# Moving the head-pair interleave of batches 3 and 4 from GpSimd to VectorE, behind the third output tile

## The chip, the cores and the metric

One core of a Trainium2 chip. The metric is the device time of one execution in microseconds (us). The engines are TensorE (PE, its weight loads PEld), VectorE (DVE), ScalarE (ACT), GpSimd (POOL), and the sync engine's queue (SP), which starts most stores.

## The reference

Attention with a decay bias over 8 batches of 8 heads, then an MLP with a gelu on the 4608 resulting tokens.

```python
scores = scale * np.matmul(q, k.transpose(0, 1, 3, 2))          # 8 x 8 x 576 x 576, head size 64
scores = np.where(causal, -1e9, scores + np.minimum(bias, 0.0)) # bias from a cumulated sum of s
attn = softmax(scores)
x = np.matmul(attn, v)   # rearranged to [4608, 512]
h = x @ w_in             # [4608, 2048]
out = gelu(h) @ w_out    # [4608, 512], float32
```

## The kernel before

The program runs in chunks c = 0 to 8 of 512 tokens; I call chunk c "stage c". Stages 1 to 6 do the MLP of chunk c and, woven into its second half, the attention of batch c + 1. They also prepare batch c + 2: its q and k come in as bf16 (`early`), are rearranged so that the two heads of a pair lie side by side (`interleave`), are stored to DRAM as rows, and are read back by transposing DMAs into `qkT`.

```python
def interleave(b, n):
    ...
    for j in range(2):
        (nc.gpsimd if b < 5 else nc.vector).tensor_copy(        # L180: 128 x 1152 bf16
            t[:, j].rearrange("g r e d -> g e r d"),
            early[b, n][:, j].rearrange("g e (r d) -> g e r d", r=G),
        )

# in stage c >= 1, nb = c + 1, pairs p of heads
late = int(c == 1)
for p in range(1, NP):
    if nb + 1 < B and p == 1 + late:
        interleave(nb + 1, "q"); write_rows(nb + 1, 0, nc.sync)
    if nb + 1 < B and p > 1 and not late:
        transpose_rows(nb + 1, p - 2)
    sc_item(nb, p)          # scores (L387), exp on ScalarE (L403), causal masks on VectorE (L412, L417)
    av_item(nb, p - 1)      # avd, avn (L425); ln on ScalarE (L441, L442); xT on VectorE (L461)
    l2_item(c, p, 0, 12)    # 24 o_ps matmuls (L544)
    if p == NP - 1:
        ...                 # the transposes left over, then:
        av_item(nb, p); norm_rest(nb)
    l2_item(c, p, 12)       # 8 more, then o_sb <- o_ps on VectorE (L551) and the store
    if nb + 1 < B and p == 1 + late:
        interleave(nb + 1, "k"); write_rows(nb + 1, 1, nc.sync)
```

The names: P is exp of a pair's scores, and its mask must be done before `avd` and `avn`, the sums over P (denominator and numerator) that give `xT`, the MLP's input; h_ps and o_ps are the MLP's first and second matmul. In front of `avd` of pair 1 or 2 stand 32 o_ps matmuls (24 and then 8 of one output tile); in front of `avd` of pair 3 only 24.

## Time and profile before

| | before |
|---|---|
| time, the three runs known before the prediction | 333.27 us median (333.2 to 333.33) |
| the profiled run | 331.73 us, span 329.8 |
| TensorE busy | 315.5 us, 96% of the span |
| VectorE, GpSimd busy | 194.6 us, 78.7 us |
| stage 1, 2, 3 in the profile | 35.29, 36.91, 34.05 us |

The profile's page gives busy times, groups of instructions by source line ("L412"), and the chain of work that ended last. A stage is measured from its first h_ps matmul to the next stage's, as the chain has them (in stage 1 this is the first one behind a wait for xT; four stand before it). Idle time counts only where it holds up TensorE.

### The profile page before, as it was taken

What the parts mean: (1) busy time and instruction counts of PE and PEld (TensorE: products, weight loads), DVE (VectorE), ACT (ScalarE), POOL (GpSimd) and SP (SyncE); (2) the same over time, 40 slices, a digit from 0 to 9 for tenths busy, and PEclk for the clock granted to TensorE, in tenths of its full rate; (3) what the DMA queues carried; (4) which work ended last, traced back from release to release, by engine and by line L of the source; (5) the groups of instructions that cost most, each with busy time, mean ns of one, the idle gap of its engine ahead of it and who ended that gap; (6) DMA issues with size and microseconds to landing.
All of it is one profiled execution on the core that took longest, in us unless ns stands there. A gap on an engine that the chain in (4) does not pass through costs nothing.

```text
span 329.8 us, 8731 instructions
## 1 busy us (share of the span) xinstructions
PE 315.5 (96%) x3755; PEld 182.8 (55%) x3755; DVE 194.6 (59%) x368; ACT 205.0 (62%) x292; POOL 78.7 (24%) x112
## 2 busy tenths in 40 slices
PE   7999998999999996999999999999999999999992
PEld 3566555666655554556655565556555655455552
DVE  5776548994589348937495658745783663150021
ACT  3796849668666855577676767677759676104400
POOL 8744254305610555007102500230000000000000
PEclk9999999999999999999999999999999999999998
DMA  7999999854975599977997995585410110010012
GB/s 111 219 208 213 231 196 265 248 107 65 273 229 113 96 230 215 181 123 224 252 150 136 211 293 104 96 242 177 109 34 34 54 45 2 34 65 34 1 66 72
DMA packets 53837, 47.45 MB, mean 144 GB/s; under 512 B 31328, under 2 KB 43872, under 8 KB 53792
## 3 DMA queue, kind: packets, MB, share of 16 engines
q0 software_dynamic: 15936, 23.07, 38.4%
q1 hardware_dynamic: 37856, 23.75, 28.6%
q8 instruction: 31, 0.51, 0.7%
q14 instruction: 14, 0.11, 0.1%
HBM read 36.85 MB, written 16.52 MB: 162 GB/s over the span
## 4 chain that ended last, share of the span: by engine, by line
PE 88%; ACT 4%; DVE 3%; issue 2%; DMA 1%; POOL 0%; DVEq 0%; POOLq 0%
PE h_ps L522 38%; PE o_ps L544 35%; PE sc_ps L387 5%; PE avn L425 3%; PE avd L425 3%; ACT P L403 2%; DMA early_q<-in_k_dram 1%; PE o_ps L565 1%; DVE qkT L372 1%; PE avr L425 1%; DVE xT L461 1%; PE tr_ps L366 1%; ACT ln L441 1%; ACT ln L442 1%; PE avw L425 0%
## 5 line engine op out<-in xcount | busy, mean ns | idle before, releaser
L544 PE MATMUL o_ps<-w_out_r,gT 128*64 128x512 bf16 x1120 | 129.3, 380 | 0.0
L522 PE MATMUL h_ps<-xT,w_in_r 128*64 128x512 bf16 x1152 | 126.2, 379 | 0.6 <-DVE xT L461 0.6
L522 PEld LDWEIGHTS <-w_in_r 128*64 128x64 bf16 x1152 | 68.5, 110 | 56.3 <-issue 1.1
L544 PEld LDWEIGHTS <-gT 128*64 128x64 bf16 x1120 | 61.0, 110 | 49.9
L529 ACT ACTIVATE gT<-h_ps 128x1024 bf16<-128x1024 f32 x54 | 54.3, 1023 | 53.9 <-PE h_ps L522 53.9
L403 ACT ACTIVATE P<-sc_ps 128x1024 bf16<-128x1024 f32 x64 | 62.0, 1021 | 26.4 <-PE sc_ps L387 24.7
L412 DVE TENSOR_TENSOR P<-P,tri_bf 128x512 bf16<-128x512 bf16 x58 | 29.5, 516 | 45.7 <-ACT P L403 45.3
L551 DVE COPY o_sb<-o_ps 128x512 f32<-128x512 f32 x33 | 22.7, 688 | 49.1 <-PE o_ps L544 49.1
L215 DVE TENSOR_REDUCE amx<-qkT 128x2 f32<-128x1152 bf16 x32 | 40.9, 1334 | 0.0
L204 POOL DMA_DIRECT2D raw_v<-in_v_dram x40 | 34.3, 880 | 7.8 <-DMA w_in_r<-in_moe_w_in_dram 2.0
L461 DVE SCALAR_TENSOR_TENSOR xT<-avn,ln 128x256 bf16<-128x256 f32 (+3 forms) x66 | 22.4, 385 | 19.6 <-ACT ln L442 14.7
L232 DVE TENSOR_TENSOR vv<-raw_v,wb 128x512 bf16<-128x512 f32 (+3 forms) x44 | 25.1, 631 | 0.0
L441 ACT ACTIVATE ln<-avd 128x256 f32<-128x256 f32 x58 | 19.2, 391 | 8.6 <-PE avd L425 8.6
L222 DVE TENSOR_REDUCE amv<-raw_v 128x1 f32<-128x2048 f32 (+1 forms) x16 | 23.0, 1469 | 2.5 <-DMA raw_v<-in_v_dram 2.5
L442 ACT ACTIVATE ln<-ln 128x512 f32<-128x512 f32 (+1 forms) x40 | 23.5, 587 | 1.3
L532 ACT ACTIVATE gT<-h_ps 128x512 bf16<-128x512 f32 x36 | 19.6, 602 | 6.3 <-PE h_ps L522 6.3
L387 PE MATMUL sc_ps<-qkT 64*128 64x256 bf16 (+2 forms) x320 | 21.1, 250 | 1.3 <-ACT P L403 0.5
L387 PEld LDWEIGHTS <-qkT 64*128 64x128 bf16 x320 | 12.9, 94 | 15.7 <-issue 12.4
L425 PEld LDWEIGHTS <-wb 128*64 128x64 bf16 x384 | 17.1, 110 | 6.5 <-issue 3.0
L425 PEld LDWEIGHTS <-vv 128*64 128x64 bf16 x384 | 17.7, 110 | 3.3 <-DVE xT L461 1.6
L425 PE MATMUL avd<-P,wb 128*64 128x256 bf16 x232 | 16.7, 263 | 2.0 <-DVE P L412 2.0
L666 POOL CAST pace<-qkT 128x1 f32<-128x1 bf16 x4 | 0.8, 196 | 69.0 <-DMA qkT<-rows 69.0
(101 smaller groups left out, 179.6 us busy)
## 6 DMA issues: line engine op xcount, KB each, us to landing
out_dram<-o_sb SPq DMA_DIRECT2D x35, 256.0 KB, 3.5
raw_v<-in_v_dram POOLq DMA_DIRECT2D x32, 256.0 KB, 9.5
rows<-qk_bf SPq DMA_DIRECT2D x12, 576.0 KB, 6.6
early_q<-in_q_dram POOLq DMA_DIRECT2D x13, 288.0 KB, 10.5
early_k<-in_k_dram POOLq DMA_DIRECT2D x13, 288.0 KB, 11.6
w_in_r<-in_moe_w_in_dram POOLq DMA_DIRECT2D x4, 512.0 KB, 11.6
w_out_r<-in_moe_w_out_dram POOLq DMA_DIRECT2D x4, 512.0 KB, 15.1
raw_v<-in_v_dram POOLq DMA_DIRECT2D x8, 128.0 KB, 9.9
```

What stands on the lines that cost most here:

```text
L204: nc.gpsimd.dma_start(out=t[:n_st, st, :, :], in_=bass.AP(tensor=v.tensor, offset=v.offset + b * H * S * D + st * 128 * D, ap=[[D, n_st], ...
L215: nc.vector.tensor_reduce(amx[:, b * NP + p], qkT[b % 2][:, :, p, :S], axis=AX, op=ALU.max, apply_absolute_value=True)
L232: eng.tensor_tensor(vb[:n_st, st0:st1, h0:h1, :], t[:n_st, st0:st1, h0:h1, :], wb[:n_st, st0:st1, b * H + h0 : b * H + h1] .unsqueeze(3).t ...
L387: nc.tensor.matmul(s_ps[:, e, off : off + n], lhsT=qkT[b % 2][e * 64 : e * 64 + 64, 1, p, jt * 128 : jt * 128 + 128], rhs=qkT[b % 2][e * 6 ...
L403: nc.scalar.activation(P[:, :, UO[u] : UO[u] + UW[u]], s_ps[:, :, : UW[u]], func=AF.Exp, scale=scale)
L412: eng.tensor_tensor(d, d, tri_bf.unsqueeze(1).unsqueeze(1).to_broadcast([128, 2, 2, 128]), op=MULT)
L425: nc.tensor.matmul(out[e * 64 : e * 64 + 64, lo : lo + n], lhsT=(wb[:, jt, b * H + h : b * H + h + 1].to_broadcast([128, 64]) if den else ...
L442: nc.scalar.activation(ln[:, :w], ln[:, :w], func=AF.Exp, scale=-1.0)
L461: nc.vector.scalar_tensor_tensor(out if p1 - p0 > 1 else out[:, 0], cut(num), math.exp(-LNC[c]), cut(ln), op0=MULT, op1=MULT,)
L522: nc.tensor.matmul(h_of[c, f2][i][e * 64 : e * 64 + 64], lhsT=w_in_r[:, ko, ft * 128 + e * 64 : ft * 128 + e * 64 + 64], rhs=xT[:, ko, c * ...
L529: nc.scalar.activation(gT_of[c][:, f2 * 2 : f2 * 2 + 2, :], hh_of[c, f2], func=AF.Gelu)
L544: nc.tensor.matmul(o_ps[e * 64 : e * 64 + 64], lhsT=gT[:, ft, t0 : t0 + 64], rhs=w_out_r[:, ft, :], start=(ft == 0), stop=(ft == FT - 1), ...
```

## The change

The intent is to take the copies of batches 3 and 4 off GpSimd, put them on VectorE at a point where it has time and the data have landed, and gather the DMA transposes behind the row stores.

```diff
-            (nc.gpsimd if b < 5 else nc.vector).tensor_copy(
+            (nc.gpsimd if b == 2 else nc.vector).tensor_copy(
...
-            late = int(c == 1)
+            late = c < 3
             for p in range(1, NP):
-                if nb + 1 < B and p == 1 + late:
+                if nb + 1 < B and p == 1 and not late:
                     interleave(nb + 1, "q")
                     write_rows(nb + 1, 0, nc.sync)
...
+                if nb + 1 < B and p == 2 and late:
+                    interleave(nb + 1, "q")
+                    write_rows(nb + 1, 0, nc.sync)
                 if nb + 1 < B and p == 1 + late:
                     interleave(nb + 1, "k")
                     write_rows(nb + 1, 1, nc.sync)
```

## The prediction

> **What bounds the kernel now.** I read the page first (busy shares, then the chain that ended last), then the windows by stage, then the chain and the timelines of the two stages that the change touches. The stages are the chunks c of the MLP; a stage starts at its first h_ps matmul (L522).
>
> ```profile
> PE 315.5 (96%) x3755; PEld 182.8 (55%) x3755; DVE 194.6 (59%) x368; ACT 205.0 (62%) x292; POOL 78.7 (24%) x112
> ...
> PE 88%; ACT 4%; DVE 3%; issue 2%; DMA 1%; POOL 0%; DVEq 0%; POOLq 0%
> ```
>
> TensorE is busy 96% of the span and carries 88% of the chain of waits. VectorE at 59% is not the bound. So only a stretch in which TensorE stands still can be won, and all of the standing still together is 329.8 - 315.5 = 14.3 us. The next table says where in the steady part it is (columns: stretch, length, busy time of each engine, clock, DMA share, GB/s). The stretches are stages c=1, 2, 3 and 5.
>
> ```profile
> 59.21:94.50 35.29, 34.51 (x422) 22.20 (x423) 25.88 (x44) 24.62 (x36) 13.07 (x16) 1.00 0.78 186
> 94.50:131.41 36.91, 34.43 (x394) 19.30 (x392) 24.67 (x36) 23.88 (x35) 13.95 (x19) 1.00 0.81 162
> 131.41:165.46 34.05, 34.05 (x395) 19.39 (x392) 21.81 (x39) 23.36 (x34) 7.03 (x10) 1.00 0.91 196
> ...
> 199.58:233.62 34.04, 34.04 (x394) 19.35 (x392) 22.01 (x41) 23.87 (x35) 4.44 (x6) 1.00 0.65 156
> ```
>
> Stages 3 and 5 do the same matmuls as stage 2 (394 or 395) in 34.05 us without a gap; they interleave their next batch on VectorE. Stage 2, which interleaves batch 4 on POOL, takes 36.91, so 36.91 - 34.05 = 2.86 us more. Stage 1 (batch 3 on POOL) has 35.29 - 34.51 = 0.78 us without a matmul; the rest of its surplus over 34.05 is work of its own, 28 more matmuls. The clock is 1.00 in all.
>
> The chain inside stage 2 and the timelines of POOL and VectorE there tell what the 2.86 us are:
>
> ```profile
> 124.04 0.95 DVE P L412
> 124.99 3.59 issue
> 128.58 0.41 DVE P L412
> 128.99 0.14 DVE P L417
> 129.13 0.68 DVE xT L461 x2
> 129.81 0.04 issue
> 129.85 0.57 PE avn L425 x8
> ```
>
> ```profile
> 123.97 2.24 POOL L180 COPY qk_bf<-early_q 128x1152 bf16<-128x1152 bf16 x2
> 126.14 2.22 POOL L180 COPY qk_bf<-early_k 128x1152 bf16<-128x1152 bf16 x2
> ```
>
> ```profile
> L412 DVE TENSOR_TENSOR P<-P,tri_bf x58: 405/425/4616, 14.7 to 264.1; 128x512 bf16<-128x512 bf16 x58
> ```
>
> The causal mask of head pair 3 (L412, median 425 ns) starts at 124.04, 0.07 us after the first POOL copy, and lasts 4616 ns, until 128.66; the four POOL copies end at 128.36. So one mask stood behind all four. TensorE then waits 2.04 us for the mask and 0.45 us for xT behind it. In stage 1 the same thing happened more mildly: the two k copies ran from 89.64 to 92.07, and within them the mask L412 at 89.98 took 1.08 us instead of 0.42 and L417 at 90.99 took 1.16 instead of 0.22. The q copies from 86.39 to 88.63 met only L461 and L551, which read PSUM, and slowed neither.
>
> [...] the blocked operations are L412 and L417 (two SBUF inputs, 4616 and 1161 ns at most), and L551 out of PSUM keeps 693 ns at most. [...] the trace has 450 to 462 as medians of L180 on VectorE. [...] the trace has 1151 ns for the same copy, 2.5 times VectorE's. [...] of VectorE's first q copies, one took 890 ns at 150.7, as POOL began to issue raw_v (150.79).
>
> **The change, part by part.**
>
> It removes 8 of the 12 POOL copies (batches 3 and 4): 8 x 1.15 = 9.2 us of POOL, none of it on the chain by itself; on the chain is what they block. It leaves the four of batch 2 (56.0 to 60.6), where a mask of 1.04 us and one of 1.16 stay slow, so that loss stays.
>
> It adds 8 copies on VectorE, four in stage 1 and four in stage 2, behind the o_sb copy of the third output tile:
>
> ```profile
> L180 DVE COPY qk_bf<-early_q x6: 450/462/890, 150.7 to 219.2; 128x1152 bf16<-128x1152 bf16 x6
> L180 DVE COPY qk_bf<-early_k x6: 449/452/491, 155.2 to 223.7; 128x1152 bf16<-128x1152 bf16 x6
> ```
>
> A pair of them takes 0.85 us on the timeline (155.18), as they overlap a little, so four take about 1.65 us.
>
> Stage 2. The o_sb copy ends at 123.35. The early tiles of batch 4 were issued from 111.12 to 113.12, the last landed 8.9 us later at 122.0, so nothing is waited for. Copies: 123.3 to 124.95. Masks, which without that would start at 124.04 and 124.95: 124.9 to 125.3 and 125.25 to 125.65, L417 until 125.8. Next comes xT of pair 2 (L461), which can't start before ScalarE's ln, 125.51 + 0.63 = 126.14. So the copies fit into time in which VectorE waits anyway, with about 0.35 us to spare; one slow copy (890) would use it up exactly. The matmul that needs the mask starts behind 24 o_ps matmuls, at 126.77. The stage should thus shrink to the 34.05 us of stage 3: a gain of 2.86, and I take 2.8.
>
> Stage 1. The o_sb copy ends at 88.38; q copies until 89.2. The last k piece was issued at 79.7 and landed 9.8 us later, at 89.5, so VectorE stands in front of k for 0.4 us. k copies: 89.55 to 90.4. Masks: 90.4 to 91.15, L417 to 91.3, xT from 91.3 (ln is ready at 91.17) to 92.1, in three pieces that took 0.81. Before, xT ended at 92.88 and avn started at 92.93. avn cannot start before its avd matmuls end, some 92.0. Gain: 92.93 - 92.15 = 0.78; with a doubt about the wait for k, I take 0.7.
>
> What moves: the row stores. Stage 1 stores k at 90.5 instead of 92.10, stage 2 stores q and k at about 124.3 and 125.2 instead of 126.24 and 128.40. In stage 2 the eight DMA transposes go together after the rows. Before, they started at 134.09, were split by a store, and the last landed by 150.26, when the pace copy on POOL ran. With k rows landing 9.8 us after 125.2 they start near 135 less the earlier shift, take some 10 to 11 us as in stage 1 (11.17), and the first pair is there by 139. The first score matmul of batch 4 was at 146.09 and will be near 142.6. It holds. The loads behind the pace copy in stage 2 move up by some 1.5 us: no cost.
>
> Sum: 2.8 + 0.7 = 3.5 us. Nothing later waits for VectorE (stages 3 to 6 have no gap), so it carries to the end: 333.27 - 3.5 = 329.8 us, 1.05% less.
>
> **The rivals.**
>
> 1. VectorE becomes the wait. Behind the third tile there is only the slack above. If [...] a tile lands late, masks slip by as much as 1 us and pair 3 starts late. For: a copy of 890 ns at 150.7, and early_k(3) landing at 89.5. Against: stages 3 to 5 carry two copies before each mask group without a gap, and POOL has no DMA issue near 88. It would leave a gain of 1.5 to 2.7: 330.6 to 331.8 us.
> 2. The gathered transposes come too late for stage 3 or block the output stores in the sync queue. For: transposes run one after another, 8 in 11.17 us. Against: rows are stored earlier than before, and three o_sb buffers covered a store held until 139.48. If it held, stage 3 would stand for 1 to 3 us, and the time would be 331 to 333.
> 3. [...] the stretched mask came from something else (say its input). Against: it ended 0.3 us after the last POOL copy, and stages with no POOL copy show none. It would leave 333.
>
> **Range and chances.** The mechanism is direct, and stage 3 shows what stage 2 becomes. If all of the idle time goes, and a little more of stage 1 than I counted, the gain is 2.86 + 0.78 = 3.64, or with rounding and scatter 4: low 329.2. If rival 1 takes a good part, 331.3. A gain over 2% would need 6.7 us, nearly twice what both stages lose: 0.01. A loss over 2% would need a new wait of 10 us: 0.01. The rest, 0.98, is within 2%.
>
> **What would show it.** Right: stage 2 at 34.0 to 34.3 us and stage 1 at 34.5 to 34.8, with no mask above 0.7 us after 62 us; the chain without the 3.59 us of "issue"; L180 with 20 copies on VectorE near 450 ns and 4 on POOL; stages 3 to 6 unchanged at 34.05. Wrong: a TensorE gap in stage 2 or 1 of over 0.5 us before avd or avn behind L412 or L461 (rival 1); one before sc_ps at the start of stage 3 behind a transpose (rival 2); a mask of 4 us with no POOL copy beside it (rival 3).

2.8 + 0.7 = 3.5 us come from the traces alone. What the traces show is that one mask stood behind four POOL copies (4616 ns, median 425); why it does is not shown. To "slowed neither": beside the q copies L461 took 425, 280 and 281 ns and L551 0.69 us; L461 at 87.25 in the changed kernel, with no POOL copy there, took 425, 280 and 278, and the median of L551 is 691 ns. I call the waiting of a mask behind POOL copies "the block".

## The result

The changed kernel took 328.63 us (median of six runs, 327.34 to 330.29), against 332.94 for the kernel before (six runs, 331.15 to 333.33). The ratio is 0.9887, 95% interval 0.9848 to 0.9927. Ratios here are the mean time of one kernel's fast runs over that of the other's of the same rounds, so not quite the ratio of the quoted medians. Executions over 1.5% slower than the fastest of the same kernel are left out of the means. The predicted 329.8 with a range from 329.2 was too high; the time lies 0.57 us below the range.

The page of the changed kernel, busy times and chain by engine:

```profile
PE 315.0 (96%) x3753; PEld 182.9 (56%) x3755; DVE 191.8 (58%) x376; ACT 204.9 (62%) x292; POOL 69.6 (21%) x104
...
PE 76%; DMA 15%; POOL 4%; ACT 2%; DVE 1%; issue 1%; DVEq 0%; POOLq 0%
```

POOL lost 9.1 us and VectorE, although it got eight more instructions, lost 2.8: its copies are short (medians of 451 and 452 ns), and its masks no longer stand blocked. The chain now runs through DMA loads of the first 50 us and through early_k of stage 1. Stages 1, 2 and 3 of the changed kernel (columns as in the prediction's table of stretches):

```profile
60.27:95.68 35.41, 34.72 (x422) 22.14 (x423) 25.52 (x48) 24.52 (x36) 8.30 (x12) 1.00 0.85 174
95.68:129.72 34.04, 34.04 (x394) 19.36 (x392) 21.40 (x39) 23.30 (x34) 9.55 (x15) 1.00 0.78 174
129.72:163.77 34.05, 34.05 (x396) 19.39 (x392) 22.39 (x40) 23.95 (x35) 7.08 (x10) 1.00 0.91 199
```

Stage 2 has lost 2.87 us: the 2.48 us without a matmul, and 0.39 us that had counted as busy. Stage 1 won nothing in this run, and its timeline shows why (first VectorE, then TensorE; the bracket is the idle time ahead and what ended it):

```profile
91.70 0.83 DVE L180 COPY qk_bf<-early_k 128x1152 bf16<-128x1152 bf16 x2 [1.52 <-DMA early_k<-in_k_dram]
```

```profile
94.11 0.57 PE L425 MATMUL avn<-P,vv 128*64 128x256 bf16 x8 [0.51 <-DVE xT L461]
```

The k piece of batch 3 landed only at about 91.5, so VectorE stood in front of it for 1.52 us and the masks came late again. It took its instructions in order: exp had ended at 90.10 and 91.01, and the two masks L412 started behind the k copies, at 92.44 and 92.78. In stage 2 the loads were in time:

```profile
124.45 0.82 DVE L180 COPY qk_bf<-early_q 128x1152 bf16<-128x1152 bf16 x2
125.19 0.85 DVE L180 COPY qk_bf<-early_k 128x1152 bf16<-128x1152 bf16 x2
125.96 0.74 DVE L412 TENSOR_TENSOR P<-P,tri_bf 128x512 bf16<-128x512 bf16 x2
126.63 0.21 DVE L417 TENSOR_TENSOR P<-P,tri_bf 128x128 bf16<-128x128 bf16 x1
127.35 0.75 DVE L461 SCALAR_TENSOR_TENSOR xT<-avn,ln 128x256 bf16<-128x256 f32 x2 [0.51 <-ACT ln L442]
```

Four copies, both masks and L417 end 0.5 us before xT could start anyway: this is where the prediction placed them. The span of this profile is only 1.6 us below that of before (328.2 against 329.8). Stage 2 gives 2.87, stage 1 takes 0.12, and stage 1 began 1.06 us later (60.27 against 59.21): in the changed kernel's run TensorE waited 0.97 us for early_k of batch 1 at 50.72, in a part that the change doesn't touch. So single profiles mislead by more than a microsecond; the experiments had to tell scatter from gain.

### The profile page after: what moved, and what is told of

It reads as the page before. It is cut to its first block, busy times and chain, and to the rows that moved or that the text cites. A ratio compares the mean times of both kernels' runs of the same rounds, so it can differ in the third digit from the quotient of the medians.

```text
span 328.2 us, 8740 instructions
## 1 busy us (share of the span) xinstructions
PE 315.0 (96%) x3753; PEld 182.9 (56%) x3755; DVE 191.8 (58%) x376; ACT 204.9 (62%) x292; POOL 69.6 (21%) x104
## 4 chain that ended last, share of the span: by engine, by line
PE 76%; DMA 15%; POOL 4%; ACT 2%; DVE 1%; issue 1%; DVEq 0%; POOLq 0%
PE h_ps L522 34%; PE o_ps L544 30%; DMA early_k<-in_k_dram 7%; DMA w_out_r<-in_moe_w_out_dram 5%; PE sc_ps L387 4%; PE avd L425 3%; PE avn L425 3%; DMA w_in_r<-in_moe_w_in_dram 3%; PE o_ps L565 1%; POOL raw_v L204 1%; PE avr L425 1%; ACT P L403 1%; POOL early_q L117 1%; POOL early_k L117 1%; POOL early_q L105 0%
## 5 line engine op out<-in xcount | busy, mean ns | idle before, releaser
L551 DVE COPY o_sb<-o_ps 128x512 f32<-128x512 f32 x33 | 22.7, 687 | 49.1 <-PE o_ps L544 49.1
L412 DVE TENSOR_TENSOR P<-P,tri_bf 128x512 bf16<-128x512 bf16 x58 | 24.6, 432 | 42.9 <-ACT P L403 42.5
L461 DVE SCALAR_TENSOR_TENSOR xT<-avn,ln 128x256 bf16<-128x256 f32 (+3 forms) x66 | 22.4, 386 | 20.5 <-ACT ln L442 14.0
L425 PE MATMUL avn<-P,vv 128*64 128x256 bf16 x232 | 16.0, 260 | 0.6 <-DVE xT L461 0.5
```

Source lines behind the costliest of these rows:

```text
L412: eng.tensor_tensor(d, d, tri_bf.unsqueeze(1).unsqueeze(1).to_broadcast([128, 2, 2, 128]), op=MULT)
L425: nc.tensor.matmul(out[e * 64 : e * 64 + 64, lo : lo + n], lhsT=(wb[:, jt, b * H + h : b * H + h + 1].to_broadcast([128, 64]) if den else ...
```

## The experiments

My theory: POOL copies hold VectorE's masks up (4616 ns in place of 425), a mask that is late by more than the matmuls ahead of `avd` makes TensorE stand, and only that is won. Rivals: the new place and the gathered transposes win it; or the engine alone, wherever the copies stand; or the long mask has nothing to do with POOL. After the result there were two more questions: is there a gain that I did not count, and what makes the kernel before scatter. All results were correct against the reference. Edits are against the changed kernel where the text doesn't say the kernel before, and are cut to what matters.

### The changed kernel again

> The changed kernel once more, for its scatter. My theory ([...] 2.87 us out of stage 2, which the profile of the changed kernel showed, and up to 0.8 us out of stage 1 where the k piece of batch 3 lands in time) expects the ratio to the kernel before at 0.987 to 0.991, stage 2 at 34.0 to 34.1 us in the new profile, and runs spread over 1 to 3 us, as the loads of the first 90 us land early or late. The rival, that there is a further lasting gain of 0.5 to 1 us that I did not count, expects a stage other than 1 and 2 to be shorter than before in this profile too.

Median 328.69 us (six runs, 327.67 to 329.43); ratio 0.9930 (0.9897 to 0.9963). Its profile, stages 1 and 2:

```profile
59.71:94.14 34.43, 34.40 (x422) 22.16 (x423) 24.90 (x46) 23.92 (x35) 8.30 (x12) 1.00 0.80 204
94.14:128.19 34.05, 34.05 (x394) 19.36 (x392) 22.00 (x42) 23.88 (x35) 9.54 (x15) 1.00 0.84 176
```

Here k had landed, and stage 1 is 34.43: 0.86 us less than in the first profile of before, against the 0.7 predicted (two more profiles of before, below, put this in doubt). No other stage is shorter than before: the rival of a further lasting gain in the changed kernel falls. The ratio lies a little above the range that I had given (0.987 to 0.991), because the kernel before was faster here (331.29 median).

### Half of the change at a time

Batch 4 alone, batch 3 left on POOL:

```diff
-            (nc.gpsimd if b == 2 else nc.vector).tensor_copy(
+            (nc.gpsimd if b in (2, 3) else nc.vector).tensor_copy(
-                if nb + 1 < B and p == 1 and not late:
+                if nb + 1 < B and (p == 2 if c == 1 else p == 1 and not late):
-                if nb + 1 < B and p == 2 and late:
+                if nb + 1 < B and p == 2 and c == 2:
```

> Batch 4 alone on VectorE behind the third tile, batch 3 as before on POOL. My theory: stage 2 at 34.05 us, 2.8 to 2.9 us less than before; stage 1 keeps its slowed masks (about 35.3 us). Time lower by 2.8 us, ratio 0.9916. Rival (the gain comes from POOL's loads or the row stores of both batches together): less than 2 us.

Median 329.20 us, ratio 0.9949 (0.9912 to 0.9986); stage 1 35.13, stage 2 34.05 us. The stages are as the theory says. The time isn't: the ratio is worth 1.7 us, where I expected 2.8 and the rival less than 2. Its interval (0.5 to 2.9 us) holds both, so only the stage lengths speak for the theory here.

Batch 3 alone, batch 4 left on POOL:

```diff
-            (nc.gpsimd if b == 2 else nc.vector).tensor_copy(
+            (nc.gpsimd if b in (2, 4) else nc.vector).tensor_copy(
-            late = c < 3
+            late = c == 1
```

> Batch 3 alone on VectorE behind the third tile, batch 4 as before on POOL. My theory: stage 1 at 34.6 to 35.4 us depending on when the k piece of batch 3 lands (0 to 0.8 us won), stage 2 still with a mask of 2 to 4.6 us and 36 to 36.9 us long; time lower by 0 to 0.8 us, ratio 0.9975 to 1.0. If the loads behind batch 3 move, POOL's copies of batch 4 move against the mask, and stage 2 may change by up to 1.5 us either way. Rival (both parts worth the same): 1.9 us.

Median 332.54 us, ratio 1.0066 (1.0024 to 1.0108): slower than before, which I had not expected. Its profiled run (330.17, the fastest) has stage 1 at 35.24, with VectorE in front of early_k for 1.35 us, and stage 2 at 36.57, with a mask of 4275 ns behind the POOL copies of batch 4. So batch 3 on VectorE is worth little by itself. Four of the six runs (one of them, 335.18, slow) had a granted clock of 0.986 to 0.991, which the profiled one (0.996) had not; the runs on the clock below bear on that, but why they are more than in before isn't shown.

### The place without the engine

```diff
-            (nc.gpsimd if b == 2 else nc.vector).tensor_copy(
+            (nc.gpsimd if b < 5 else nc.vector).tensor_copy(
```

> The new places in program order, with the engine as before (POOL for batches 3 and 4 too). My theory: [...] POOL reaches the copies when its queue of loads lets it, so stage 2 keeps a mask of 2 to 4.6 us and stays at 36 to 37 us; time within 0.8 us of before, ratio 0.998 to 1.002. Rival (it is the place and the gathered transposes that won): 3 to 4 us lower, as with the whole change.

Ratio 1.0022 (0.9973 to 1.0071), median 330.74: no gain, so neither the place nor the gathered transposes win anything by themselves. Its profile, of the fastest of the six runs, taught more than I expected from it. Stage 1 was as short as in the best profile of the changed kernel, with batch 3 on POOL:

```profile
59.32:93.75 34.43, 34.40 (x422) 22.21 (x423) 25.75 (x42) 23.92 (x35) 13.09 (x16) 1.00 0.81 205
```

Its POOL copies ran from 83.70 to 88.5 and met the masks of pair 2, and the 32 matmuls covered that. In stage 2, POOL's queue let the copies of batch 4 start at 118.08, and so they met the mask of pair 2 (timelines of VectorE and of TensorE):

```profile
118.28 4.81 DVE L412 TENSOR_TENSOR P<-P,tri_bf 128x512 bf16<-128x512 bf16 x2 [0.69 <-ACT P L403]
```

```profile
122.91 0.60 PE L425 MATMUL avd<-P,wb 128*64 128x256 bf16 x8 [0.49 <-DVE P L412]
```

The block is as long as in the kernel before, but TensorE waited 0.49 us in place of 2.04, as pair 2 has 32 o_ps matmuls ahead of its avd. Stage 2 took 35.34. The copies started there as POOL's issue of early_k ended (117.48 and 0.61 us); in the kernel before, the same issue ended at 123.97. On POOL it is thus left to POOL's queue, and the loads that it waits for, which mask is hit.

### The kernel before, profiled twice more

> The kernel before, profiled again. In the run with the new places on POOL the copies of batch 4 fell on the mask of pair 2, which has 32 o_ps matmuls in front of the matmul that needs it, and stage 2 took 35.3 us; in the first profile of before they fell on the mask of pair 3, which has 24, and it took 36.9. My theory: the scatter of before (328.99 to 335.12 us) comes in part from where POOL's queue lets its copies fall, so stage 2 of this profile is anywhere from 34.1 to 38 us, and always with a mask of 1 to 4.7 us beside the POOL copies. Rival: stage 2 is 36.9 again and all scatter lies in the first 60 us.

> The same once more: stage 2 at 34.1 to 38 us with the place of the POOL copies; rival: 36.9 us in each profile.

333.74 and 332.60 us. In both, the copies hit a mask of pair 3 (4383 and 4705 ns), so my guess that the place would differ was not borne out here. Stage 1 took 35.19 and 34.63 us: before reaches by itself most of what the changed kernel's better profile has (34.43). But something else differed. TensorE's gap ahead of avd was 2.41 and 2.13 us, and behind it the granted clock fell to 0.50 for some 3.4 us, an estimate from the averages of the stretches (in the second profile 0.74, 0.50 and 0.89 in 128.15:130, 130:132 and 132:134). Stretches of the first of these two (clock is the third number from the end; 0.84 and 0.59 are averages over both states):

```profile
124.00:129.20 5.20, 2.79 (x30) 1.48 (x27) 4.71 (x4) 1.90 (x4) 4.84 (x5) 1.00 1.20 187
129.20:131.90 2.70, 2.25 (x30) 1.36 (x31) 1.70 (x6) 2.24 (x6) 0.00 (x0) 0.84 1.15 277
131.91:135.00 3.09, 3.09 (x18) 1.31 (x16) 3.09 (x7) 1.01 (x1) 0.00 (x0) 0.59 0.90 319
135.00:138.00 3.00, 3.00 (x30) 1.59 (x28) 3.00 (x4) 1.70 (x2) 0.00 (x0) 1.00 1.16 87
```

In the first profile of before, with a gap of 2.04 us, the same place reads:

```profile
130.00:132.00 2.00, 2.00 (x32) 1.28 (x30) 1.21 (x4) 1.92 (x5) 0.00 (x0) 1.00 1.12 295
132.00:134.00 2.00, 2.00 (x22) 1.03 (x20) 2.00 (x4) 0.78 (x1) 0.00 (x0) 1.00 1.11 349
```

Stages 2 and 3 together took 73.00 and 72.62 us in these two profiles, 70.96 in the first, and 68.09 in the changed kernel. The same block thus cost 2.87 us in one run and 4.5 to 4.9 in others. Over the 42 later runs of the kernel before (328.99 to 335.12 us, median 331.5), 37 count as fast (three are slow, two profiled singly): five with a mean clock of 0.989 to 0.990 averaged 332.8 us, the 32 with 0.993 or more 331.0. The three slow ones, 334.68 to 335.12 us, have 0.990 or 0.991, so leaving them out of the ratios makes before look a little faster than it is. Of twelve runs of the changed kernel none had less than 0.994.

### POOL copies made twice

The kernel before, with the four copies of batch 4 repeated on POOL:

```diff
-        for j in range(2):
+        for j in (0, 1) * (2 if b == 4 else 1):
```

> The kernel before, with the four POOL copies of batch 4 made twice (the second time the same data into the same place). My theory, that a mask that starts after the first copy stands behind all copies that follow one another: one mask of 8.5 to 9.2 us (4.6 plus four copies of 1.15, less what it starts late), stage 2 4 to 4.6 us longer than the same place of the copies gives in before: 39 to 41.5 us. Rival (the mask waits for something that is not the POOL copies, its input or a slot): its length stays near 4.6 us.

The group of L412 in this profile (min/median/max in ns) and its two masks of pair 2:

```profile
L412 DVE TENSOR_TENSOR P<-P,tri_bf x58: 407/425/9428, 14.5 to 268.6; 128x512 bf16<-128x512 bf16 x58
```

```profile
118.65 9.76 DVE L412 TENSOR_TENSOR P<-P,tri_bf 128x512 bf16<-128x512 bf16 x2 [0.69 <-ACT P L403]
```

One mask of 9.4 us, twice the 4.6, a little over the range that I gave. Here the mask waited for the POOL copies, all of them that followed one another; the rival that it waits for its input falls. TensorE's gap was 5.44 us, the clock 0.50 in the 3.8 us behind it, stage 2 took 41.8 us (39 to 41.5 expected), the time was 336.56.

### The engine without the place

The kernel before, with VectorE for batches 3 and 4 at the old places:

```diff
-            (nc.gpsimd if b < 5 else nc.vector).tensor_copy(
+            (nc.gpsimd if b == 2 else nc.vector).tensor_copy(
```

> VectorE for batches 3 and 4, at the places of before in program order. My theory: VectorE runs in order, and there the loads have not landed: q of batch 3 stands in front of pair 2's masks with its last piece landing some 3.5 us later, q of batch 4 in front of pair 1's masks with 5 us to wait. Stage 1 at 35 to 37 us, stage 2 at 37 to 41 us, time 2 to 5 us over before (ratio 1.005 to 1.016). Rival (the engine alone makes the gain, the place is of no account): ratio near 0.99.

> VectorE at the old places, profiled again. The first profile (328.95 us, the fastest of four) had q of batch 4 landing only 1.3 us after VectorE got to it, which was hidden. In the slower runs I expect the loads later and VectorE in front of them for 3 to 6 us, a TensorE gap of 1 to 3 us before avd or avn in stage 1 or 2. Rival: no gap there, and the time lost elsewhere.

> VectorE at the old places once more: as in the run before this one, a TensorE gap of 1 to 3 us before avd or avn in stage 1 or 2 where the loads land late; rival: no gap there, and the time lost elsewhere.

Four timed runs from 328.95 to 333.57, median 331.93, ratio 1.0018 (0.9962 to 1.0074); the loss that I expected at least (1.005) was not reached. (That VectorE runs in order is read from the result's profile, where masks with their P ready at 90.10 and 91.01 started at 92.44 and 92.78.) The profile of the fastest has no gap in stages 1 and 2: q of batch 4 landed 1.33 us after VectorE got to it, and the matmuls ahead covered that. The two further profiles (334.93 and 331.67 us) show the other case. In the first of them:

```profile
119.54 0.97 DVE L180 COPY qk_bf<-early_q 128x1152 bf16<-128x1152 bf16 x2 [6.27 <-DMA early_q<-in_q_dram]
```

```profile
120.98 0.96 PE L425 MATMUL avd<-P,wb 128*64 128x256 bf16 x8 [3.44 <-DVE P L412]
```

VectorE stood 6.27 us in front of q of batch 4, TensorE 3.44 us behind it, and the clock was 0.50 from 121 to 127. In the second, 4.07 and 1.27 us, and the matmuls slowed behind this short gap too: 32 of o_ps took 5.33 us instead of 3.62, as with a clock of 0.50 for some 3.4 us (an estimate, twice the 1.71 us lost):

```profile
118.36 0.59 PE L425 MATMUL avd<-P,wb 128*64 128x256 bf16 x8 [1.27 <-DVE P L412]
```

```profile
120.00 5.33 PE L544 MATMUL o_ps<-w_out_r,gT 128*64 128x512 bf16 x32
```

So the engine alone removes the block and puts a wait for the loads in its place; the later place is what makes the engine pay. Which loads land when, and why, I didn't pursue.

### The same delay without POOL

The changed kernel, with each VectorE copy of batch 4 made three times:

```diff
-        for j in range(2):
+        for j in (0, 1) * (3 if b == 4 else 1):
```

> The changed kernel, but each VectorE copy of batch 4 made three times, so that 8 more copies of 0.41 us, 3.3 us, stand in front of the masks of pair 3 in stage 2, with no POOL copy there. Theory: what counts is how late that mask ends, whatever made it late. The masks end near 3.3 us later than in the changed kernel, TensorE waits 2 to 2.5 us, stage 2 is 36 to 37 us as in before; and if the gap of TensorE is what lowers the granted clock afterwards in some runs of before, then some of these six runs have a clock of 0.991 or lower and none of the changed kernel's has. Ratio 0.998 to 1.004. Rival (a POOL copy itself slows TensorE or the rest): stage 2 stays under 35 us. Rival on the clock (the dip comes from elsewhere): all six clocks at 0.994 or higher.

Ratio 1.0012 (0.9968 to 1.0056), median 331.39 us, the time of before. Stage 2 took 36.40, with the masks of pair 3 late by the added copies and this wait (2 to 2.5 us expected), the clock 1.00 behind it:

```profile
129.36 0.60 PE L425 MATMUL avd<-P,wb 128*64 128x256 bf16 x8 [1.51 <-DVE P L412]
```

So the cost is how late the mask is, whatever makes it late. One of six runs had a clock of 0.990 and was the slowest (333.59).

### A longer gap, empty and filled

The same with five copies each; and again with 21 matmuls on PSUM that nothing reads, ahead of the avd that waits:

```diff
+                    if c == 2:
+                        fill = ps.tile([128, 2, 512], fp32, tag="sc", bufs=2, name="fill")
+                        for _ in range(21):
+                            nc.tensor.matmul(fill[:, 0], lhsT=busy[:, :128], rhs=busy, start=True, stop=True)
                     av_item(nb, p)
```

> The changed kernel with each VectorE copy of batch 4 made five times: 16 more copies, 6.6 us in front of the masks of pair 3 in stage 2. The 8 more of the earlier run made a gap of 1.51 us, so this one should make one of some 4.8 us. If a gap lowers the clock, the longer one should do it in most or all runs: mean clock 0.984 to 0.992, and behind the gap some 3 us at about half speed, so stages 2 and 3 together 5.1 us (gap and xT behind it) plus 1.3 to 1.8 us longer than the changed kernel's 68.1. Time near 335 us. Rival (the dip is not tied to the gap): clock 0.994 or higher in most of the six runs, stage 3 at 34.05.

> The same, with 21 matmuls of 128x512 that nothing uses in front of the matmuls that wait (21 of 0.216 us, 4.5 us), so TensorE hardly stands still though the masks come as late. If the gap lowers the clock: all clocks at 0.994 or higher, stage 2 as long as without the fill until the gap ends, but no slow matmuls after it; 1.3 to 1.8 us faster than delay5. Rival: the same clock as delay5 and no faster.

| | empty gap | filled gap |
|---|---|---|
| median, range of six runs | 335.18 (334.28 to 339.30) | 333.27 (333.01 to 334.05) |
| granted clock of the six runs | 0.985, 0.985, 0.985, 0.994, 0.986, 0.989 | 0.995 to 0.999 |
| ratio to before | 1.0117 (1.0067 to 1.0167) | 1.0074 (1.0030 to 1.0118) |
| stages 2 and 3 in the profile | 75.59 us | 73.43 us |

Behind the empty gap of 4.50 us the profile has this stretch, its clock at half:

```profile
131.33:134.60 3.27, 3.19 (x30) 2.00 (x32) 1.89 (x7) 2.19 (x6) 0.00 (x0) 0.50 1.13 289
```

The 0.216 us of the expectation is the distance of two such matmuls (`warm`) in the changed kernel's profile, which start at 5.914 and 6.130 us; here the 21 took 4.63 us, 0.22 each. With the fill, TensorE's timeline has no gap ahead of avd, and no slow matmul after it:

```profile
125.94 4.71 PE L751 MATMUL fill<-busy 128*128 128x512 bf16 x20
130.57 0.57 PE L425 MATMUL avd<-P,wb 128*64 128x256 bf16 x8
```

The masks come equally late in both, and useless work makes the kernel 1.9 us faster. This shows that the gap itself lowers the clock afterwards. It doesn't do so each time: one of the six runs with the empty gap kept 0.994. The other kernels agree. In the 42 runs of the six kernels in which batch 4 holds up no mask or the gap is filled (the changed one, batch 4 alone, the fill, and the three below) no clock was under 0.994; in 21 of the 68 runs of the others (8 of 40 of before) it was 0.991 or less.

### Towards a better version

Batch 2 is still on POOL. Moving its copies to VectorE, behind the last pair of batch 1:

```diff
-            interleave(2, "q")
-            interleave(2, "k")
...
             av_item(1, 3, rest=False)
+            for i, n in enumerate("qk"):
+                interleave(2, n)
+                write_rows(2, i, nc.sync)
```

(The engine is now VectorE for every batch, and two older write_rows calls of batch 2 go.)

> Batch 2 as well on VectorE, its copies and row stores behind the last pair of batch 1. Theory: the masks of 1.04 and 1.16 us at 56 to 58 us fall to 0.42 and 0.22, xT of pair 2 comes some 0.9 us earlier and the first h_ps matmul of stage 1 with it; the rows of batch 2 are stored about where they were, so the loads of batch 3 stay where they are and VectorE waits longer for k in stage 1. Net gain over the changed kernel 0 to 0.9 us, ratio to before 0.986 to 0.992. Rival: rows and loads come late and stage 1 loses more than stage 0 wins.

Median 329.30, ratio 0.9933 (0.9897 to 0.9968): no gain over the changed kernel (0.9930 and 0.9887 in its two sets), and above the 0.986 to 0.992 that I expected. The masks of stage 0 are short again (426 ns at most), but in the profile stage 1 began at 60.86 and lasted 34.93: TensorE waited for early loads of batch 1 and then for xT behind k of batch 3.

The other weak spot is VectorE in front of k of batch 3. Moving only that interleave behind xT of pair 2:

```diff
                 av_item(nb, p - 1)
+                if c == 1 and p == 3:
+                    interleave(nb + 1, "k")
+                    write_rows(nb + 1, 1, nc.sync)
                 l2_item(c, p, 0, 12)
...
-                if nb + 1 < B and p == 1 + late:
+                if nb + 1 < B and c > 1 and p == 1 + late:
                     interleave(nb + 1, "k")
```

> The changed kernel with the k interleave of batch 3 moved behind xT of pair 2, where its last piece has landed. Theory: VectorE no longer stands in front of k; stage 1 is at 34.4 to 34.6 us in each profile (the two profiles of the changed kernel had 35.41 and 34.43); mean gain over the changed kernel 0.3 to 0.7 us, within noise; no mask of pair 3 late. Rival: the later k rows delay the transposes, and stage 2 starts late with sc_ps.

Median 328.62, ratio 0.9919 (0.9885 to 0.9953); stage 1 34.42. As expected, within noise of the changed kernel. And both together:

> Both of these together. Theory: 0.6 to 1.6 us under the changed kernel (328.7), so 327 to 328 us, ratio to before 0.981 to 0.990; stage 1 at 34.4 to 34.6 us. Rival: loads and rows, later by what is won, take it back: no lower than the changed kernel.

Median 327.34 us, six runs from 327.17 to 327.42, ratio 0.9889 (0.9860 to 0.9919), the lowest of this set and 1.3 us under the changed kernel's median. The masks and stage 1 in its profile:

```profile
L412 DVE TENSOR_TENSOR P<-P,tri_bf x58: 406/424/426, 14.5 to 259.7; 128x512 bf16<-128x512 bf16 x58
```

```profile
58.52:92.95 34.43, 34.40 (x422) 22.21 (x423) 26.49 (x50) 24.34 (x36) 6.91 (x10) 1.00 0.78 171
```

No mask of the whole kernel exceeds 426 ns. The spread of 0.25 us, against 3 us for the changed kernel, suggests that what is left of the scatter there came through the two waits removed here; I only argue that, since it rests on one set of runs.

## Why the prediction was right or wrong

It was wrong: 328.63 us lies 0.57 us under the range, which ended at 329.2. What failed is the base and the scatter in "333.27 - 3.5 = 329.8" and "with rounding and scatter 4: low 329.2". The mechanism held in stage 2.

- **The cause (the block): right.** Doubling the POOL copies doubled it (4616 to 9428 ns), and neither the place alone nor a cause outside POOL explains the gain. In stage 1 masks did get in between two copies (1.08 and 1.16 us in the first profile of before); what decides this the runs don't show.
- **Stage 2, 2.8 us: right** for the run that was profiled: 36.91 to 34.04 and 34.05. VectorE's copies fitted in the idle time worked out for them. (A slip in the sum: a copy of 890 ns instead of 450 takes 0.44 us, more than the 0.35 to spare, and not "exactly" that.)
- **Stage 1, 0.7 us: not shown.** The loss that it was read from is real in that one profile. But before had 35.29, 35.19 and 34.63 us in three profiles, POOL at the new place 34.43, and the changed kernel 35.41 and 34.43, as k landed 1.5 us after VectorE reached it or in time. "With a doubt about the wait for k" was the place; the doubt was larger than the 0.1 that I took off, and the 35.29 it was taken from was the longest of the three. The two kernels that move k further back had 34.42 and 34.43.
- **"The clock is 1.00 in all": a premise that failed.** It was true of that one run. In a part of the runs of before the gap also halved the clock for about three microseconds (0.50 for some 3.4 us in the two later profiles), and the same block cost 4.5 to 4.9 us in place of 2.87. The sum has no term for this.
- **"333.27 - 3.5 = 329.8" and "low 329.2": the step that put the number out.** I took the gain from a profile of 331.73 us off a median of other, slower runs. Off its own run the sum gives 331.73 - 3.5 = 328.2, and the twelve runs of the changed kernel average 328.7. And I left under 0.4 us for rounding and scatter, where the three runs of before had spread over 0.13 us: later runs of the same kernel spread over 6 us, and six of the changed one over 2.95. The gain itself was 3.75 us between the averages of the first set (332.64 and 328.89) and about 2.3 in the second, so 3.5 lies inside its scatter. What the three runs at 333.2 to 333.33 had lost beyond the profiled one stays open: their clocks are not known, and later runs reached 333 both with a clock of 0.990 and, once, with 0.999.
- **The rivals.** The first, VectorE as the new wait, is what happened in stage 1 through a late load: TensorE stood 0.51 us before avn, just over the sign of 0.5 that the prediction had set. The other half of this rival, POOL's DMA work in front of the copies, was small there. (The copy of 890 ns started at 151.08; the one at 150.7 took 450.) In all 18 profiles, the 247 copies on VectorE during which POOL did nothing took 461 ns at most, and all 35 that took more than 500 ns met a DMA issue of POOL; in stage 2 of the changed kernel the longest took 490. The second rival, late transposes, didn't happen in either profile of the changed kernel. The third fell.
- **Under 2%: right**; the two sets of runs give 1.1% and 0.7%.

## What to carry to other kernels

When an engine's average is far from full, look at its longest single instruction, and at what another engine did meanwhile: 4.6 us of one mask did not show in any busy share. VectorE took its instructions in order, so moving work to it paid only behind the point where the data had landed (at the old places it stood up to 6.27 us in front of a load, ratio 1.0018; at the new ones 0.9887 and 0.9930): choose the engine and the place together. Take a predicted gain off the time of the run from which it was read, and leave a range as wide as the runs scatter. Count a gap of TensorE as possibly costing more than its length: behind gaps of 2.13 and 2.41 us ahead of avd the clock was 0.50 for some 3.4 us, which is 1.7 us more as an estimate (half of 3.4), and behind one of 1.27 us 32 matmuls took 1.71 us longer. Behind gaps of 1.51, 1.70 and 2.04 us, with the same second one of 0.45 us ahead of avn as those three, the matmuls were not slower, so the length alone doesn't decide; behind 3.44, 4.50 and 5.44 us the clock was 0.50 in the profiles.
